# Attention through a small memory, fused with a two-layer ReLU-squared network: batches 2 to 7 form memory and scores for eight heads at once

## The chip, the cores and the metric

The kernel runs on one core of a Trainium2 chip. The metric is device time in microseconds; three runs of the kernel before gave 746.95, 749.21 and 749.82, median 749.21.

## What is computed

```
a    = softmax over the 576 tokens of phi              # 8 batches, 8 heads, 32 memories
k_m  = einsum('bhsm,bhsd->bhmd', a, k)                 # 32 x 64 for each head
v_m  = einsum('bhsm,bhsd->bhmd', a, v)
attn = softmax over the 32 memories of (q @ k_m^T / 8)
x    = attn @ v_m, heads side by side                  # 4608 x 512
out  = (relu(x @ w_in) ** 2) @ w_out                   # 512 -> 2048 -> 512
```

All inputs and the output are float32.

## The kernel before

Two products carry nearly all of the work. The attention output is never formed: `vw` (line 754) multiplies the value memory with the rows of `w_in` of each head, and `mm1` (line 864) multiplies the result with the attention weights of a batch, which gives the hidden layer directly. `mm2` (lines 899, 900, 902) and `mm2_left` (line 925, the tokens left over) multiply the squared hidden layer with `w_out`. These main products run in fp32r on high and low parts: `ath`/`atl`, `gh`/`glo`, and two parts of `w_out`. A program float32 matmul stands as two records in the trace, an fp32r one as one.

The small products run in plain float32. In batches 2 to 7 `memory(b, hh)` works on four heads at a time, so twice per batch. 128 partitions hold four tokens each, and 64 of them one more; `fold` takes the maximum and later the sum over these in three DVE instructions (lines 562 to 564). A transpose (570), a DVE maximum (572) and a second transpose (573) give the maximum over all tokens, which DVE subtracts (574); ACT takes the exponential (576). Line 594 sums over the tokens, line 582 forms keys and values in 128x32 tiles of TensorE, four at a time, over five groups of tokens (20 matmuls of 128 columns). After scaling, two transposes (625, 629) turn the result into `kb` and `VT`. One tile `KV` holds the inputs of a half; it is loaded again for each half. `scores` (793) then runs four times per batch, for four heads and 256 or 320 tokens each: two matmuls in 128x64 tiles.

Batches 0 and 1 use another form of the scores (`attention_turned`) and share the decoding of the weights with it. They run first, while the inputs and the weights are loaded. Their first main product waits for all of this; until then PE is kept busy with `idle` matmuls of zeros (`fill`, line 454).

The whole program is written down as a list of operations with their tiles. `Plan.order` then lets a planner put each operation on an engine and in an order. It counts with costs per operation and ranks taken from the table `PLACES` for the first operations and from its own rounds for the rest. What comes out is fixed: each engine runs its own list in order, SP too, which issues all loads. An operation whose input isn't there holds up all that stands behind it on its engine. PSUM has four banks `acc`, two `h`, and one each `pa` and `pv`; `vw` takes `pa` and `pv`, memory and scores of batches 2 to 7 take `pa` alone.

Of the kernel before, what the change touches and what calls it, by code (L numbers as in the profile page):

```python
# [20 lines left out]
P = 128  # L21
# [16 lines left out]
AHEAD = 2000  # L38
BEGIN = {"PE": 1000.0, "DVE": 1100.0, "ACT": 800.0, "POOL": 2100.0, "SP": 800.0}
# [79 lines left out]
class Buf:  # L119


    def __init__(self, plan, tag, slot, make, before):
        self.plan, self.tag, self.slot, self.make, self.before = plan, tag, slot, make, before
        self.tile = None
        self.users = []
        self.written = {}
        self.read = {}
        self.closed = False

    def __call__(self):  # L130
        if self.tile is None:
            self.tile = self.make()
        return self.tile


class Op:
    __slots__ = ("ways", "fn", "deps", "users", "late", "cap", "left", "start", "gap", "lead", "port", "size", "seq", "slack", "code")


class Plan:  # L140

    def __init__(self):
        self.ops = []
        self.slots = {}
# [205 lines left out]
def tt(n):  # L355
    return 68 + 1.04 * n
# [714 lines left out]
```

## Time and profile before

| | |
|---|---|
| median of three runs | 749.21 us |
| the profiled execution | 749.23 us, its span 747.3 us |
| PE busy | 733.1 us (98%) |
| DVE busy | 513.4 us (69%) |
| ACT busy | 311.1 us (42%) |
[...]
| moved by DMA | 66.38 MB |

Matmuls overlap, so the time that one takes from the next is read from start to start: in an undisturbed run of fp32r matmuls of 512 columns that is 0.231 us, of 256 columns 0.120, of 320 columns 0.146.

### The profile page before, as it was taken

The numbers are of one execution on the slowest core, as the hardware profiler recorded it, in microseconds if no ns is written. First come the engines' busy times: TensorE is split into PE (matmuls) and PEld (weight loads), VectorE is DVE, ScalarE is ACT, GpSimd is POOL, SyncE is SP. The second block draws the span as 40 slices with busy tenths as digits, with TensorE's granted clock in tenths as the row PEclk, the third lists the DMA queues.
The fourth block names the chain that finished last, engine by engine and source line by source line (L and its number), as shares of the span: only waits on it lengthen the run. The fifth ranks groups of instructions, "written<-read, shape, count | busy, mean of one in ns | idle before, by whom it ended". The sixth has DMA issues, their size and how long they took to land.

```text
span 747.3 us, 13089 instructions
## 1 busy us (share of the span) xinstructions
PE 733.1 (98%) x5004; PEld 586.9 (79%) x5009; DVE 513.4 (69%) x1200; ACT 311.1 (42%) x723; POOL 56.6 (8%) x132
## 2 busy tenths in 40 slices
PE   7899999999999999999999999999999999999997
PEld 4568888888878887788868888687877888788886
DVE  4889998944677677846767666955677576775551
ACT  3467997845422323523423323423242342443320
POOL 2000000010010000400014000120003200040000
PEclk9999999999999999999999999999999999999999
DMA  9994545260640036400363015410344102220002
GB/s 235 239 255 115 167 145 144 89 172 16 171 148 17 1 81 152 104 1 1 106 154 90 1 52 135 105 46 1 80 115 120 36 1 65 61 58 0 1 1 70
DMA packets 59997, 66.38 MB, mean 89 GB/s; under 512 B 18400, under 2 KB 48096, under 8 KB 59936
## 3 DMA queue, kind: packets, MB, share of 16 engines
q1 hardware_dynamic: 55904, 56.77, 30.0%
q0 software_dynamic: 3552, 8.13, 4.2%
q8 instruction: 39, 0.64, 0.4%
q10 hardware_dynamic: 480, 0.66, 0.4%
q14 instruction: 22, 0.18, 0.1%
HBM read 56.10 MB, written 9.44 MB: 88 GB/s over the span
## 4 chain that ended last, share of the span: by engine, by line
PE 92%; DMA 1%; ACT 0%; DVE 0%; issue 0%; ACTq 0%
PE h L864 28%; PE acc L899 16%; PE acc L902 16%; PE acc L900 16%; PE accl L925 6%; PE vwpv L754 4%; PE psc L793 2%; PE pkv L582 2%; DMA raw<-in_moe_w_out_dram 1%; PE psc L710 1%; PE pq L682 0%; PE vwpa L754 0%; PE pvt L625 0%; PE pvt L629 0%; PE pkv L594 0%; PE pmx L570 0%
## 5 line engine op out<-in xcount | busy, mean ns | idle before, releaser
L864 PE MATMUL h<-ath,vw 128*128 128x320 f32 (+1 forms) x1024 | 208.9, 298 | 0.9 <-ACT r L868 0.9
L899 PE MATMUL acc<-wo,gh 128*128 128x512 f32 x512 | 205.4, 401 | 0.0
L900 PE MATMUL acc<-wo,gh 128*128 128x512 f32 x512 | 201.0, 393 | 0.0
L864 PEld LDWEIGHTS h<-ath,vw 128*128 128x128 f32 x1024 | 168.6, 189 | 29.2 <-issue 7.2
L902 PE MATMUL acc<-wo,glo 128*128 128x512 f32 x512 | 159.9, 399 | 0.0
L870 ACT ACTIVATE gh<-r 128x512 fp32r<-128x512 f32 x128 | 81.0, 633 | 151.3 <-DVE r L869 116.2
L899 PEld LDWEIGHTS acc<-wo,gh 128*128 128x128 f32 x512 | 96.3, 188 | 28.2 <-issue 8.1
L902 PEld LDWEIGHTS acc<-wo,glo 128*128 128x128 f32 x512 | 91.9, 189 | 24.7 <-issue 7.5
L900 PEld LDWEIGHTS acc<-wo,gh 128*128 128x128 f32 x512 | 96.5, 188 | 17.2
L864 PE MATMUL h<-atl,vw 128*128 128x320 f32 (+1 forms) x512 | 109.5, 295 | 0.0
L869 DVE TENSOR_SCALAR r<-h 128x256 f32<-128x256 f32 (+1 forms) x104 | 47.4, 456 | 75.2 <-PE h L864 74.4
L868 ACT ACTIVATE r<-h 128x256 f32<-128x256 f32 (+1 forms) x152 | 61.2, 410 | 89.2 <-PE h L864 80.3
L874 DVE TENSOR_TENSOR glo<-r,gh 128x512 fp32r<-128x512 f32 x128 | 88.0, 687 | 13.7 <-ACT r L872 9.7
L864 PEld LDWEIGHTS h<-atl,vw 128*128 128x128 f32 x512 | 82.3, 189 | 0.0
L873 DVE TENSOR_TENSOR r<-r 128x576 f32<-128x576 f32 x69 | 52.2, 757 | 28.9 <-ACT gl L871 26.4
L961 POOL DMA_DIRECT2D out_dram<-o x84 | 41.4, 501 | 195.8 <-ACT o L428 187.4
L925 PE MATMUL accl<-wo,gl 128*128 128x512 f32 x192 | 48.0, 396 | 0.0
L925 PEld LDWEIGHTS accl<-wo,gl 128*128 128x128 f32 x192 | 35.5, 188 | 11.5 <-issue 4.0
L872 ACT ACTIVATE r<-r 128x576 f32<-128x576 f32 x59 | 40.5, 686 | 1.2
L754 PE MATMUL vwpv<-wi,VT 64*32 64x512 f32 (+1 forms) x264 | 34.9, 588 | 0.7 <-DVE wi L510 0.7
L754 PE MATMUL vwpa<-wi,VT 64*32 64x512 f32 (+1 forms) x264 | 34.9, 588 | 0.0
L871 ACT ACTIVATE gl<-r 128x64 fp32r<-128x64 f32 x128 | 31.5, 246 | 4.8 <-DVE r L869 4.5
(133 smaller groups left out, 700.9 us busy)
## 6 DMA issues: line engine op xcount, KB each, us to landing
raw<-in_moe_w_out_dram SPq DMA_DIRECT2D x16, 512.0 KB, 3.6
KV<-in_v_dram SPq DMA_DIRECT2D x16, 512.0 KB, 5.6
KV<-in_k_dram SPq DMA_DIRECT2D x16, 512.0 KB, 4.3
raw<-in_moe_w_in_dram SPq DMA_DIRECT2D x32, 256.0 KB, 4.3
q<-in_q_dram SPq DMA_DIRECT2D x24, 304.0 KB, 4.4
q<-in_q_dram SPq DMA_DIRECT2D x24, 240.0 KB, 3.9
out_dram<-o POOLq DMA_DIRECT2D x80, 64.0 KB, 2.0
phi<-in_phi_dram SPq DMA_DIRECT2D x16, 256.0 KB, 5.7
```

The lines of the kernel that those rows point to most:

```text
L754: nc.tensor.matmul(ps_[hh]()[32 * s:32 * s + 32, 0:n], V()[pr, s, :], W()[pr, s, c0:c0 + n], start=True, stop=True, tile_position=(64 * hh ...
L864: nc.tensor.matmul(p()[:, 0:n], V()[:, l, hh, c0:c0 + P], x()[:, hh, cs], start=(i == 0), stop=(i == 5))
L868: op({"ACT": act(n), **({} if b < 2 else {"DVE": tt(n)})}, lambda e, cs=cs, n=n, p=p: nc.scalar.activation(r()[:, cs], p()[:, 0:n], AF.Rel ...
L869: else nc.vector.tensor_scalar(r()[:, cs], p()[:, 0:n], 0.0, None, ALU.max), [p], [(r, h)])
L870: op({"ACT": act(SM)}, lambda e: nc.scalar.activation(gh(), r()[:, 0:SM], AF.Square), [r], [gh])
L873: else nc.vector.tensor_mul(r(), r(), r()), [r], [r], port=BOTH)
L874: vec({"DVE": tt(SM)}, lambda e: nc.vector.tensor_sub(glo(), r()[:, 0:SM], gh().bitcast(F32)), [r, gh], [glo])
L899: nc.tensor.matmul(a(), gh()[:, c], t()[:, 0], start=f0, stop=False)
L900: nc.tensor.matmul(a(), gh()[:, c], t()[:, 1], start=False, stop=False)
L902: nc.tensor.matmul(a(), glo()[:, c], t()[:, 0], start=False, stop=f1)
L925: nc.tensor.matmul(a(), G()[:, l, :], t()[:, w], start=(ff == 0 and n == 0), stop=(ff == NFF - 1 and n == 2))
L961: d(rows, o()[32 * j:32 * (j + n), :])
```

## The change

Memory of batches 2 to 7 takes all eight heads in one go. 64 partitions hold heads 0 to 3, the other 64 hold heads 4 to 7, nine tokens to a partition. Keys and values are formed in 64x32 tiles, eight at a time, over nine groups of tokens, in two instalments (five groups, then four) that share the one tile `KV`. Maximum and sum over the nine tokens are one DVE instruction each, which reads with a stride of 32 elements. The second transpose of the maximum becomes two matmuls in 128x64 tiles (`spread`). One pair of transposes yields keys and values of all heads. Scores take eight matmuls in 64x32 tiles with 288 tokens, twice per batch. They use `pa` and `pv`. The loads of q go to 32 partitions each, four to a tile. `mm1` cuts its 576 tokens into 288 and 288, not 256 and 320. The old memory function stays for batches 0 and 1 as `memory_half`, with keys and values as separate products of 64 columns and the maximum in one DVE instruction.

The planner's rounds go: ranks for all operations come from one table (its rows are not shown), and its cost of a PE operation now has a term for a change of tile shape (`SWITCH`) as well as other figures.

```diff
@@ order
-        rank = {o: PLACES[o.seq] * 10.0 if o.seq < len(PLACES) else best[1][o] for o in self.ops}
-        for _ in range(ROUNDS):
-            found = self.forward(rank)
...
+        rank = {o: PLACES[o.seq] for o in self.ops}
+        self.last, start, engine, gap = self.forward(rank)
@@ forward
+                t += SWITCH[mode][o.mode]
+                mode = o.mode
@@ sizes
-    CUT = (0, 8, NC)
-    TOK = (slice(0, 256), slice(256, S))
+    HC = NC // 2
+    RC = S // 64
+    KC = 5
+    TOK = (slice(0, S // 2), slice(S // 2, S))
@@ memory of batches 2 to 7
+    def rows(d, dst, src, lo, hi):
+        w = src.shape[3]
+        for x in (0, 1):
+            d(dst[64 * x:64 * x + 64].rearrange("p h c w -> p h (c w)"),
+              src[0, 4 * x:4 * x + 4].rearrange("h (p c) w -> p h (c w)", c=RC)[:, :, lo * w:hi * w])
+    def memory(b):
+        A = st([P, 4 * RC * M], F32, "phi", f"phi{b}")
...
+        vec({"DVE": tt(4 * RC * M)}, lambda e: nc.vector.tensor_reduce(
+            mx().rearrange("p (h m) -> p h m", h=4), a().rearrange("p h c m -> p h m c"), AX.X, ALU.max), [A], [mx], port=None, lead=True)
...
+        def spread(e):
+            for x in (0, 1):
+                nc.tensor.matmul(pm()[64 * x:64 * x + 64, P:2 * P], mc()[:, x].broadcast_to([P, 64]), ident, start=True, stop=True, tile_position=(0, 64 * x))
...
+        def sums(e):
+            for x in (0, 1):
+                pr = slice(64 * x, 64 * x + 64)
+                nc.tensor.matmul(pk[x]()[:, SUM:SUM + 1], asum()[pr], ones[pr], start=True, stop=True, tile_position=(64 * x, 0))
+        def products(pairs, lo, hi):
+            for c in range(lo, hi):
+                for h in range(4):
+                    for x in (0, 1):
+                        pr = slice(64 * x, 64 * x + 64)
+                        for o, src in pairs:
+                            nc.tensor.matmul(pk[x]()[32 * h:32 * h + 32, o], a()[pr, h, c, :], src(pr, h, c - lo),
+                                             start=(c == 0), stop=(c == RC - 1), tile_position=(64 * x, 32 * h))
...
+        for lo, hi in ((0, KC), (KC, RC)):
+            KV = st([P, 8 * KC * D], F32, "KV", f"KV{b}_{lo}")
...
@@ scores
+    def scores(b):
...
+            for y in (0, 1):
+                Q = st([P, 2, HC, D], F32, "q", f"q{b}_{h}_{y}")
...
+            pq = [pt(x + ".0", f"psc{x}{b}_{h}") for x in ("pa", "pv")]
+            def mm(e, qT=qT, pq=pq):
+                for s in range(4):
+                    for hh in (0, 1):
+                        pr = slice(64 * hh, 64 * hh + 64)
+                        nc.tensor.matmul(pq[hh]()[32 * s:32 * s + 32, 0:32 * HC], kb()[pr, 0, s, :], qT()[pr, s].rearrange("p c t -> p (c t)"),
+                                         start=True, stop=True, tile_position=(64 * hh, 32 * s))
```

PE, where batch 2 forms keys and values, before: after six `h` matmuls of the batch in progress stand the sum (594) and the twenty products of the first half (582); a second such block for the other heads follows 41 rows later.

```order
L864 MATMUL h_1_2280<-ath_366,vw_6_2098 128x320 x2
L594 MATMUL pkv_0_2288<-ones,asum_0_2272 128x1
L582 MATMUL pkv_0_2288<-KV_0_1970,phi_0_626 32x128 x20
L902 MATMUL acc_4_0_2123<-wo_1451,glo_2201 128x512
L902 MATMUL acc_4_3_2059<-wo_1399,glo_2248 128x512
```

The same place now: `pa` holds heads 0 to 3 and `pv` heads 4 to 7, and forty products of the first five groups take turns between the two banks.

```order
L916 MATMUL h_1_2347<-ath_380,vw_6_2157 128x288 x2
L565 MATMUL pkv_pa<-ones,asum_2336 128x1
L565 MATMUL pkv_pv<-ones,asum_2336 128x1
L573 MATMUL pkv_pa<-KV_0_2044,phi_881 32x128
L573 MATMUL pkv_pv<-KV_0_2044,phi_881 32x128
L573 MATMUL pkv_pa<-KV_0_2044,phi_881 32x128
L573 MATMUL pkv_pv<-KV_0_2044,phi_881 32x128
```

The products of the last four groups stand after 7.3 us of main products, counted at the start-to-start times above (7.2 to 7.6 in the six batches). From `spread` to the sums it is 4.7 to 8.7 us.

PE at the first scores of batch 2, before: two matmuls for the first 256 tokens of four heads, and after some main products two for the next 320.

```order
L900 MATMUL acc_4_3_2059<-wo_1771,gh_2402 128x512
L793 MATMUL psc_0_0_2491<-qT_0_0_1999,kb_2350 64x256 x2
L902 MATMUL acc_4_3_2059<-wo_1771,glo_2419 128x512
L864 MATMUL h_0_2497<-ath_366,vw_7_2174 128x256 x2
L864 MATMUL h_0_2497<-atl_378,vw_7_2174 128x256 x2
```

Now eight matmuls stand together for 288 tokens of all heads.

```order
L954 MATMUL acc_4_3_2159<-wo_1868,glo_2498 128x512
L848 MATMUL pscpa_0_2539<-qT_0_2076,kb_2524 32x288
L848 MATMUL pscpv_0_2541<-qT_0_2076,kb_2524 32x288
L848 MATMUL pscpa_0_2539<-qT_0_2076,kb_2524 32x288
L848 MATMUL pscpv_0_2541<-qT_0_2076,kb_2524 32x288
...
L916 MATMUL h_0_2550<-ath_380,vw_7_2271 128x288 x2
```

Four score places of a batch became two; between the two stand 8.3 to 9.9 us of main products, and between the second and the first `vw` 1.6 to 2.1.

SP, the loads around batch 2's last q, before: the inputs of one half of batch 3 (k, v, then phi), then the q tiles of batch 2's second half.

```order
L533 DMA KV_0_1970<-in_k_dram 128x4x256
L534 DMA KV_0_1970<-in_k_dram 64x4x64
L533 DMA KV_0_1970<-in_v_dram 128x4x256
L534 DMA KV_0_1970<-in_v_dram 64x4x64
L533 DMA phi_1_2453<-in_phi_dram 128x4x128
L534 DMA phi_1_2453<-in_phi_dram 64x4x32
L784 DMA q_1_0_2508<-in_q_dram 64x2x480 x2
L784 DMA q_1_1_2557<-in_q_dram 64x2x608 x2
```

Now (KV_5 is the second instalment of batch 2, KV_0 the first of batch 3, q_1_1 the last q tile of batch 2):

```order
L838 DMA q_1_0_2167<-in_q_dram 32x2x544 x4
L533 DMA KV_5_2419<-in_k_dram 64x4x256 x2
L533 DMA KV_5_2419<-in_v_dram 64x4x256 x2
L533 DMA KV_0_2510<-in_v_dram 64x4x320 x2
L533 DMA phi_2519<-in_phi_dram 64x4x288 x2
L533 DMA KV_0_2510<-in_k_dram 64x4x320 x2
L838 DMA q_1_1_2574<-in_q_dram 32x2x544 x4
```

The last q tile of a batch, 0.56 MB, moved behind 1.90 MB of the next batch (before 1.48 MB).

## Rows read from the trace of the kernel before

**Rows 1.** The page, busy time of each engine, share and instructions.

```profile
PE 733.1 (98%) x5004; PEld 586.9 (79%) x5009; DVE 513.4 (69%) x1200; ACT 311.1 (42%) x723; POOL 56.6 (8%) x132
```

**Rows 2.** Windows: stretch, length, busy time of PE, PEld, DVE, ACT, POOL, clock, DMA.

```profile
0.00:60.00 60.00, 50.97 (x606) 33.55 (x612) 45.49 (x118) 31.15 (x66) 5.56 (x23) 1.00 1.04 236
60.00:700.00 640.00, 639.10 (x4174) 517.71 (x4173) 449.20 (x1045) 271.07 (x636) 51.05 (x109) 1.00 0.30 79
700.00:747.30 47.30, 42.99 (x228) 35.61 (x226) 18.69 (x39) 8.89 (x23) 0.00 (x0) 1.00 0.10 28
```

**Rows 3.** PE by line: count, busy us, mean ns, idle before (zeros and transposes).

```profile
L454 PE MATMUL idle<-zero 128*128 128x512 bf16 x66 | 19.6, 428 | 1.5 <-DVE ones L444 1.0 <-issue 0.3
```

**Rows 4.** PE timeline at a transpose of the maximum: start, duration, instruction.

```profile
262.05 0.27 PE L573 MATMUL pmx<-ident,mc 128*128 128x128 f32 x1
262.08 0.47 PE L899 MATMUL acc<-wo,gh 128*128 128x512 f32 x1
262.39 0.40 PE L900 MATMUL acc<-wo,gh 128*128 128x512 f32 x1
```

**Rows 5.** PE timeline at keys and values of one half of batch 3.

```profile
266.71 0.28 PE L594 MATMUL pkv<-ones,asum 128*128 128x1 f32 x2
266.92 1.30 PE L582 MATMUL pkv<-KV,phi 128*32 128x128 f32 x40
268.15 1.19 PE L902 MATMUL acc<-wo,glo 128*128 128x512 f32 x4
269.18 0.39 PE L899 MATMUL acc<-wo,gh 128*128 128x512 f32 x1
```

**Rows 6.** PE timeline at scores of 256 tokens.

```profile
282.71 0.40 PE L902 MATMUL acc<-wo,glo 128*128 128x512 f32 x1
283.04 0.65 PE L793 MATMUL psc<-qT,kb 128*64 128x256 f32 x4
283.62 0.50 PE L899 MATMUL acc<-wo,gh 128*128 128x512 f32 x1
283.96 0.40 PE L900 MATMUL acc<-wo,gh 128*128 128x512 f32 x1
```

**Rows 7.** PE timeline at scores of 320 tokens.

```profile
286.14 0.76 PE L793 MATMUL psc<-qT,kb 128*64 128x320 f32 x4
286.83 0.56 PE L864 MATMUL h<-ath,vw 128*128 128x320 f32 x2
287.23 0.45 PE L864 MATMUL h<-atl,vw 128*128 128x320 f32 x2
```

**Rows 8.** PE timeline at a vw block: sixteen records in 64x32 tiles.

```profile
302.13 0.39 PE L900 MATMUL acc<-wo,gh 128*128 128x512 f32 x1
302.45 0.61 PE L754 MATMUL vwpv<-wi,VT 64*32 64x512 f32 x1
...
303.47 0.50 PE L899 MATMUL acc<-wo,gh 128*128 128x512 f32 x1
303.81 0.40 PE L900 MATMUL acc<-wo,gh 128*128 128x512 f32 x1
```

**Rows 9.** PE timeline at the start-up: forty records of one column.

```profile
42.11 0.51 PE L591 MATMUL pkv<-ones,phi 128*32 128x1 f32 x40
```

**Rows 10.** DVE and ACT by line: batches 0 to 7, three steps of memory and scores.

```profile
L574 DVE TENSOR_TENSOR phi<-phi,pmx 128x640 f32<-128x640 f32 x16 | 13.0, 815 | 4.2 <-PE pmx L573 4.1
L805 DVE TENSOR_REDUCE red_None<-S 128x18 f32<-128x576 f32 x12 | 9.0, 751 | 0.3
L576 ACT ACTIVATE phi<-phi 128x640 f32<-128x640 f32 x16 | 11.8, 740 | 40.9 <-DVE phi L574 30.9 <-issue 9.8
```

**Rows 11.** DMA of 266 to 276 us: issues, KB each, median us to landing.

```profile
KV<-in_k_dram SPq DMA_DIRECT2D x1, 512.0 KB, 4.7
```

**Rows 12.** DMA of 0 to 58 us in sum, then PE where batch 1's last q lands.

```profile
DMA packets 16283, 14.03 MB, mean 242 GB/s; under 512 B 5220, under 2 KB 14237, under 8 KB 16277
57.95 1.04 PE L682 MATMUL pq<-ident,q 128*128 128x128 f32 x8
```

More of the change, by code (lines that the diff above doesn't have):

```diff
@@ L38 @@
 AHEAD = 2000
+SWITCH = (
+    (0, 10, 85, 85, 85),
+    (90, 0, 85, 85, 85),
+    (100, 60, 0, 85, 85),
+    (100, 60, 85, 0, 85),
+    (100, 60, 85, 85, 0),
+)
 BEGIN = {"PE": 1000.0, "DVE": 1100.0, "ACT": 800.0, "POOL": 2100.0, "SP": 800.0}
@@ L136 @@
 class Op:
-    __slots__ = ("ways", "fn", "deps", "users", "late", "cap", "left", "start", "gap", "lead", "port", "size", "seq", "slack", "code")
+    __slots__ = ("ways", "fn", "deps", "users", "late", "cap", "left", "start", "gap", "lead", "port", "size", "seq", "slack", "code", "mode")
 class Plan:
@@ L199, in order @@
     def order(self):
-        for o in reversed(self.ops):
-            e = min(o.ways, key=o.ways.get)
-            cost = FIRST + o.size / WIRE + LANDS[e] if o.size else o.ways[e] + LAT[e]
-            late = min((u.late for u in o.users), default=1e9)
-            if o.cap is not None:
-                late = min(late, o.cap)
-            o.late = late - cost
-        rank = {o: o.late - (LEAD if o.lead else 0) for o in self.ops}
-        best = None
-        for _ in range(ROUNDS):
-            found = self.forward(rank)
-            if best is None or found[0] < best[0]:
-                best = found
-            rank = self.backward(found)
-        rank = {o: PLACES[o.seq] * 10.0 if o.seq < len(PLACES) else best[1][o] for o in self.ops}
-        for _ in range(ROUNDS):
-            found = self.forward(rank)
-            if found[0] < best[0]:
-                best = found
-            rank = self.backward(found)
-        self.last, start, engine, gap = best
+        rank = {o: PLACES[o.seq] for o in self.ops}
+        self.last, start, engine, gap = self.forward(rank)
         for o in self.ops:
@@ L428, in copy, with dma @@
         nc.scalar.copy(o, i) if e == "ACT" else ENG[e].tensor_copy(o, i)
-    def dma(fn, size, r=(), w=(), eng="SP", two=False, **more):
+    def dma(fn, size, r=(), w=(), eng="SP", two=False, issue=None, **more):
         e = {"SP": nc.sync, "ACT": nc.scalar, "POOL": nc.gpsimd}[eng]
-        issue = 700 if eng == "POOL" else 1250 if two else 620
+        issue = issue or (700 if eng == "POOL" else 1250 if two else 620)
         return op({eng: issue}, lambda _: fn(e.dma_start), r=r, w=w, size=size, **more)
@@ L587, in sums @@
-        def sums(e):
-            if asum is None:
-                for c in range(SC):
-                    for s in range(4):
-                        nc.tensor.matmul(pk()[32 * s:32 * s + 32, 2 * D:2 * D + 1], a()[:, s, c, :], ones,
-                                         start=(c == 0), stop=(c == SC - 1), tile_position=(0, 32 * s))
-            else:
-                nc.tensor.matmul(pk()[:, 2 * D:2 * D + 1], asum()[:, 0:P], ones, start=True, stop=True)
-        op({"PE": 180 if asum else 530}, sums, [asum or A], [pk], lead=True, code=4 if asum else 82)
@@ L629, in memory, with mm @@
-        op({"PE": 60}, lambda e: nc.tensor.transpose(pv()[:, 0:P], two(1), ident), [kx if b < 2 else (kx, 1)], [(pv, 0)], lead=True)
-        pr = slice(64 * hh, 64 * hh + 64)
-        op({"ACT": act(P), "DVE": tt(P)}, lambda e: copy(e, VT[b]()[pr].rearrange("p h m -> p (h m)"), pv()[pr, 0:P]), [(pv, 0)], [(VT[b], hh)], lead=True)
+        def mm(e, i):
+            for c in range(SC):
+                for s in range(4):
+                    nc.tensor.matmul(pk()[32 * s:32 * s + 32, i * D:i * D + D], a()[:, s, c, :], kv()[:, i, s, c, :],
+                                     start=(c == 0), stop=(c == SC - 1), tile_position=(0, 32 * s))
@@ new lines, in memory_half @@
+        for i in (0, 1):
+            op({"PE": 700}, lambda e, i=i: mm(e, i), kin + [(KV, i), (KV, "pad")], [(pk, i)], lead=True, code=82, mode=3)
+            op({"ACT": act(P), "DVE": 75 + 1.04 * P}, lambda e, i=i: nc.scalar.activation(kx()[:, i], dup(i), AF.Copy, scale=rs()[:, 0:1]) if e == "ACT"
+               else nc.vector.tensor_scalar_mul(kx()[:, i], dup(i), rs()[:, 0:1]), [(pk, i), rs], [(kx, i)], lead=True)
+        pv = pt(bank, f"pvt{u}")
+        kb = kTs[b, hh] = st([P, 4, 2, M], F32, "kb", f"kb{u}", 2)
@@ new lines, in memory_half @@
+        op({"POOL": 250}, lambda e: nc.gpsimd.memset(kb(), 0.0), [], [kb], lead=True)
+        two = lambda i: kx()[:, i].rearrange("p r d -> p (r d)")
+        op({"PE": 30}, lambda e: nc.tensor.transpose(pv()[:, P:2 * P], two(0), ident), [(kx, 0)], [(pv, 1)], lead=True, mode=1)
+        for x in (0, 1):
+            pr = slice(64 * x, 64 * x + 64)
+            op({"ACT": act(P), "DVE": tt(P)}, lambda e, x=x, pr=pr: copy(e, kb()[pr, :, x, :], pv()[pr, P:2 * P].rearrange("p (h m) -> p h m", h=4)),
+               [(pv, 1), kb], [(kb, x)], lead=True)
@@ L633, in attention_turned @@
+        vt = VT[b][0]
+        po = slice(64 * hh, 64 * hh + 64)
+        op({"PE": 30}, lambda e: nc.tensor.transpose(pv()[:, 0:P], two(1), ident), [(kx, 1)], [(pv, 0)], lead=True, mode=1)
+        op({"ACT": act(P), "DVE": tt(P)}, lambda e: copy(e, vt()[po].rearrange("p h m -> p (h m)"), pv()[po, 0:P]), [(pv, 0)], [(vt, hh)], lead=True)
     def attention_turned(b):
@@ L816, in attention, with load @@
-    def attention(b, split=False):
-        S_ = [scores(b, hh, split) for hh in (0, 1)]
-        i = b % 2 if b < 2 else (b + 1) % 2
+            qT = st([P, 4, HC, 32], F32, "qT", f"qT{b}_{h}")
+            for y in (0, 1):
+                Q = st([P, 2, HC, D], F32, "q", f"q{b}_{h}_{y}")
+                def load(d, Q=Q, h=h, y=y):
+                    for hh in (0, 1):
+                        src = q[b, 4 * hh + 2 * y:4 * hh + 2 * y + 2].rearrange("a (p c) d -> p a (c d)", c=NC)
+                        for x in (0, 1):
+                            lo = h * HC * D + 32 * x
+                            d(Q().rearrange("p a c d -> p a (c d)")[64 * hh + 32 * x:64 * hh + 32 * x + 32, :, 0:HC * D - 32], src[:, :, lo:lo + HC * D - 32])
+                dma(load, P * 2 * (HC * D - 32) * 4, [], [Q], issue=2500, lead=True)
+                vec({"DVE": 48 + 1.13 * 64 * HC}, lambda e, qT=qT, Q=Q, y=y: nc.vector.transpose(qT()[:, 2 * y:2 * y + 2], Q()[:, :, :, 0:32]), [Q], [(qT, y)], port=None, lead=True)
@@ L819, in attention @@
+        return S_
+    def attention(b):
+        S_ = scores(b)
+        i = (b + 1) % 2
         ah, al = att[b] = (st([P, 2, S], F32R, f"ath{i}", f"ath{b}"), st([P, 2, S], F32R, f"atl{i}", f"atl{b}"))
```

308 lines of the change are left out of this document (120 added, 188 removed), and 212 rows, old and new, of the table PLACES.

## The prediction

> **What bounds the kernel now.** I read the busy times first: PE 733.1 of 747.3 us, DVE 513.4, ACT 311.1 [rows 1]. Then where PE is not busy: 9.0 us of the first 60, 0.9 us of the next 640, 4.3 us behind the last matmul [rows 2]. The granted clock is 1.00 in every stretch. In the first 60 us the DMA engines are full (share 1.04), and 66 matmuls of zeros, 19.6 us busy, stand in for work [rows 2, 3]. So there are two regimes. In the start-up the loads set the time, at 242 GB/s [rows 12]. From 60 us on nothing but PE's own instructions does, and a microsecond less on PE is a microsecond less of the span, as long as nothing else becomes late. The profiled execution took 749.23 us, its span 747.3; the median of the three runs is 749.21, so the sum is made from 749.2. A measurement of this kernel tells a change from none at about 0.5%, 3.7 us.
>
> **PE work removed in batches 2 to 7.** Costs are taken from start to start, over the 0.231 us (512 columns) or 0.146 us (320) that a main product takes undisturbed.
> A transpose: 262.05 to 262.39 is 0.34, less 0.23, so 0.11 us [rows 4].
> Keys and values of one half: 266.71 to 269.18 is 2.47, less four times 0.231, so 1.54 us, of which 0.11 is the sum (a transpose's price) and 1.43 the twenty products [rows 5].
> Scores of 256: 282.71 to 283.96 is 1.25, less two times 0.231, so 0.79 us [rows 6]. Its wait ahead is 0.33 less 0.23, 0.10.
> Scores of 320: 286.14 to 287.23 is 1.09, less 0.29 for the two main products, plus the same 0.10 ahead, so 0.90 us [rows 7].
> A vw block: 302.13 to 303.81 is 1.68, less 0.46, so 1.22 us for 512 columns [rows 8].
> All of these lie on one line: 0.37 us for each block plus 1.66 ns for each column streamed through a tile (0.79 for 256, 0.90 for 320, 1.22 for 512; 0.37 + 640 x 1.66 ns = 1.43 for five groups of 128). It holds for 128x32, 128x64 and 64x32 tiles alike, so the number of tiles that run beside each other is free, and 64x32 tiles do eight at a time in a vw block.
> Before, per batch: 8 transposes 0.88, two halves of keys and values 3.08, scores 2 x 0.79 + 2 x 0.90 = 3.38. Sum 7.34 us.
> After: one transpose 0.11; `spread`, 128 columns in two tiles, 0.58; two transposes at the end 0.22; five groups 1.43; four groups, 512 columns, 1.22; scores twice 288 columns, 2 x 0.85 = 1.70. The sums now have a tile shape of their own, 64x128: between 0.11, as before, and 0.31, with a change of shape on each side at the 0.10 of rows 6; I take 0.2. Sum 5.46 us. So 1.9 us less per batch, over six batches **11.3 us**.
> Bounds: no row has eight tiles with only 128 columns in each. If all sixteen records of a group hide behind its 0.21 us of columns, the price stands. The nearest row for the issue of short records is forty of one column, busy 0.51 us [rows 9], 12.8 ns each; sixteen at that rate are 0.20 us, just under the 0.21 us. At worst I allow a tenth more per group, 0.2 us per batch, 1.2 us in all. `spread` has as its nearest row from below the transpose that it replaces, 0.11: 2.8 us the other way.
> `mm1` in 288 and 288 columns instead of 256 and 320 streams the same columns with the same count of matmuls: nothing.
>
> [...]
>
> **Loads of batches 2 to 7.** Two of them stand closer to their use. A lone load of 0.52 MB landed 4.7 us after its issue [rows 11]; at 242 GB/s [rows 12] 2.2 us of that is the data, 2.5 fixed.
> The second instalment of keys and values, 1.05 MB, can only be issued when the first block has read the tile: 2.5 + 4.3 = 6.8 us later it is there. PE has 7.2 to 7.6 us of main products between the blocks and 0.2 us of changes of shape. Nothing, with 0.6 us to spare.
> The last q tile stands on SP behind 1.90 MB for the next batch, which start when the second block has read `KV` and `phi`. The 2.46 MB land 2.5 + 10.2 = 12.7 us after that block. Score 2 starts, by the order and the prices above, 13.1 to 14.8 us after it. Between stand a DVE transpose of 576 elements (0.73 us, scaled from the subtraction's 0.815 for 640 [rows 10]) and 0.3 us that I allow for handovers: it must land by 12.1 to 13.8. Over the five batches that have a successor that is late by 0, 0.6, 0, 0.6, 0.5: 1.7 us. But the 242 GB/s hold 5220 packets of 16283 under 512 B [rows 12], and the new loads have none (1,024 to 2,176 B). At 260 GB/s nothing is late. I take **0.8 us**, bounds 0 and 1.7 at these rates; slower loads are a rival.
>
> **The chain from `spread` to the sums.** DVE subtracts 1152 elements, ACT takes the exponential, DVE sums. Scaled from rows 10 that is 0.815 x 1.8 + 0.740 x 1.8 + 0.751 x 2 = 4.3 us, an upper figure since each has a fixed part; main products of 4.7 to 8.7 us cover it. The strided sum has no row. As fast as the contiguous one it costs nothing; at twice its time, 1.5 us more, four of the six batches (4.7 to 5.3 us of cover) would lose 0.5 to 1.1 us each, 3.5 us. I take 0.3 us for this and the waits for `pa` and `pv`: between score 2 and `vw` 1.6 to 2.1 us cover two DVE transposes of 288 elements (0.4 us each, scaled from rows 10) and the handovers. Behind a late sum stand PE's main products, which nothing else can overtake.
> DVE loses some 140 instructions; PE waited for it nowhere after 60 us [rows 2], so that gives nothing.
>
> **Start-up.** By SP's order the last load that batch 1 waits for, its second q, came after 12.98 MB and now comes after 13.50 (two `w_in` pieces went ahead of it). PE took it up at 57.95 [rows 12], so now at 60.1 (0.52 MB at 242 GB/s is 2.2 us). Ahead of it PE had 5.7 us of main products and now has 7.2. Net 0.7 us lost. Keys and values in separate products of 64 columns cost between -0.3 (bound by issue, 0.51 each) and +1.3 us per half for batches 0 and 1; mostly this lies in time that PE spends waiting for loads. I take **0.7 us** for all, bounds -1.5 and 3.
> The end is the same 48 matmuls, an evacuation and a store: the 4.3 us stay.
>
> **Sum.** 749.2 - 11.3 + 0.8 + 0.3 + 0.7 = **739.7 us**.
>
> **Rivals.**
> Late loads, moderate. The loads to 64 and 32 partitions run at some 210 GB/s: the q tile lands 14.2 us after the block, late by 1.1, 2.1, 0.4, 2.1 and 2.0, and the second instalment by 0.1 in six batches. That is 8.3 us in place of the 0.8, so 747: no change. For it: these loads have more issues (four for a q tile, before two). Against it: loads to 64 partitions were part of the 242.
> Late loads, strong, the other side. The place is the same q tile and the second instalment. From about 205 GB/s downwards the two together eat the gain; at 170 GB/s the tile lands 17.0 us after the block, on the mean 4.3 us late in five batches, and the second instalment 1.3 us late in six: 29 us, so 768. Against it: no stretch of full DMA in the trace is that slow.
> Floor per record, from the issue side. If a record costs twice the 12.8 ns of the row of forty because eight tiles need twice the weight loads of four, sixteen are 0.41 us, the nine groups 3.7 instead of 1.9, 10.6 us in all: 751, no change. Against it: the sixteen records of a vw block follow the same line as the others [rows 8].
> A better start-up. The new order may cut into the 19.6 us of zeros instead of adding to them: 3 us less, and no late loads, 736.
>
> **Chances.** Forecast 0.70 (736 to 743.5 on its own terms); better start-up 0.13; moderate lateness 0.09; floor per record 0.04; strong lateness 0.04. Faster by over 0.5% takes the forecast, the better start-up and a third of the moderate case, 0.86; the same is the rest of that case and the floor, 0.10; slower is the strong lateness, 0.04. The range 735.0 to 744.5 takes in the bounds of the sum (a saving of 10 to 13, lateness of 0 to 1.7, start-up -1.5 to 3) short of all of them at once.
>
> **What would show it.** Right: per batch one block of 40 program products of about 1.4 us and one of 32 of about 1.2, two score blocks of 0.85, PE busy from 60 us on with under 3 us idle, the first q wait of batch 1 near 60 us, and no idle time of PE behind DVE's strided sum. Wrong: idle time of PE ended by a load of q or KV, blocks of keys and values above 2 us, or more than 36 us of zeros and idle time ahead of 62 us.

## The result, and the profile after

| | before | after |
|---|---|---|
| median of the runs | 749.52 us (4 runs, 746.95 to 750.04) | 759.14 us (4 runs, 756.92 to 760.97) |
| ratio, 95% interval | | 1.0139 [1.0113, 1.0166] |
| profiled execution, its span | 749.23, 747.3 | 756.92, 755.1 |

The forecast was 739.7 us, faster by 9.5. The kernel became slower by 1.4%. The profiled executions differ by +7.7 us.

The page of after, busy time of each engine, against [rows 1]:

```profile
PE 731.2 (97%) x5637; PEld 582.4 (77%) x5641; DVE 499.4 (66%) x1062; ACT 322.4 (43%) x742; POOL 53.7 (7%) x116
```

PE is busy 1.9 us less than before, in a span 7.8 us longer. Two of the windows of [rows 2], and two short ones (stretch, length, busy time of PE, PEld, DVE, ACT, POOL, clock, DMA share, GB/s):

```profile
0.00:60.00 60.00, 48.09 (x719) 31.43 (x724) 43.17 (x100) 28.32 (x62) 4.84 (x18) 0.94 0.88 231
60.00:700.00 640.00, 631.93 (x4663) 507.58 (x4662) 434.12 (x919) 283.87 (x658) 48.81 (x98) 1.00 0.32 80
20.80:24.20 3.40, 2.54 (x42) 1.87 (x32) 2.28 (x8) 1.33 (x5) 1.09 (x3) 0.50 1.07 235
51.60:54.90 3.30, 3.30 (x36) 3.11 (x27) 0.38 (x1) 2.22 (x8) 0.00 (x0) 0.50 0.92 305
```

Two things are new. Between 60 and 700 us PE is idle for 8.1 us, where it was idle for 0.9. And in the start-up there are two stretches with a granted clock of 0.50, where each window of [rows 2] has 1.00. In the second PE is busy all of the time; ahead of it, it stood still for 2.6 us (below).

What ended PE's waits in after, over the whole span (instruction, releaser: idle us, times, longest):

```profile
PE pscpa L848 <- DVE qT L841: 4.0, 3, 2.0
PE h L916 <- issue: 2.6, 1, 2.6
...
PE acc L954 <- DVE glo L926: 2.2, 3, 1.2
```

The first is the score block of a late q tile. The second has no releaser: a stop in the first products of `h`, at 47 us. The third is a main product that waits for its input.

Where the time went I read at equal work: the times at which both kernels have as many main products (`h`, `acc`, `accl`, 3264 in each) behind them. After is 2.2 us late at its first (46.39 us), 5.2 at 80 us, about 7.1 at 150 us (neighbouring products differ by about 1 us there, as their order differs) and 8.2 at the last. From 150 us on the batches' own products, and what PE waits for them, are measured as in the prediction, from start to start over the undisturbed spacing:

| term, us | forecast | measured |
|---|---|---|
| small products of batches 2 to 7 | -11.3 | -9.9 |
| waits of score blocks (6.3) and second key and value block (1.8) | +0.8 | +8.1 |
| chain to the sums | +0.3 | +0.6 |
| `acc` waits for `glo` | 0 | +2.2 |
| start-up, to 150 us | +0.7 | +7.1 |
| tail | 0 | -0.3 |
| sum (the spans differ by 7.9) | -9.5 | +7.8 |

**The work is nearly as small as forecast.** PE by line and form, keys and values of heads 0 to 3 in batches 2 to 7 (176 to 755 us; count, busy us, mean ns, idle before):

```profile
L573 PE MATMUL pkv_pa<-KV,phi 64*32 64x128 f32 x432 | 16.2, 273 | 0.1
```

With as many records for heads 4 to 7 that is nine groups of sixteen per batch; before, two halves took five groups each. One score block without a wait, the first of batch 3 (PE timeline: start, us, instruction; sixteen records in all):

```profile
290.96 0.40 PE L952 MATMUL acc<-wo,gh 128*128 128x512 f32 x1
291.29 0.43 PE L848 MATMUL pscpa<-qT,kb 64*32 64x288 f32 x1
...
291.93 0.53 PE L916 MATMUL h<-ath,vw 128*128 128x288 f32 x2
292.30 0.43 PE L916 MATMUL h<-atl,vw 128*128 128x288 f32 x2
```

0.33 us to the block less 0.23 for the main product, 0.64 for the block, and 0.37 less 0.27 for the return: 0.84 us, forecast 0.85. The two `h` halves of 288 take 0.133 us each, together what 256 and 320 took.

**The second block of the same batch waits for q.** PE (the product behind the second key and value block, then the score block), then DVE, then SP's queue in the stretch before it:

```profile
288.45 0.50 PE L954 MATMUL acc<-wo,glo 128*128 128x512 f32 x1
...
301.54 0.43 PE L848 MATMUL pscpa<-qT,kb 64*32 64x288 f32 x1
...
303.53 0.43 PE L848 MATMUL pscpa<-qT,kb 64*32 64x288 f32 x1 [1.30 <-DVE qT L841]
304.15 0.51 PE L954 MATMUL acc<-wo,glo 128*128 128x512 f32 x1
```

```profile
302.70 0.78 DVE L841 STREAM_TRANSPOSE qT<-q 128x576 f32<-128x576 f32 x1 [3.92 <-DMA q<-in_q_dram]
```

```profile
288.60 1.25 SPq L533 DMA_DIRECT2D phi<-in_phi_dram  x2
...
292.94 2.55 SPq L838 DMA_DIRECT2D q<-in_q_dram  x4
```

The second key and value block ends at 288.45. At once SP starts the next batch's `phi` and `KV`, 1.9 MB, and only then this batch's last q. It lands at 302.62, DVE turns it, and the block takes 2.61 us instead of 0.65. Its four DMA issues (KB each, us to landing), and the window in which the DMA engines are full:

```profile
q<-in_q_dram SPq DMA_DIRECT2D x4, 136.0 KB, 8.5
```

```profile
291.00:301.00 10.00, 10.00 (x66) 8.09 (x65) 7.25 (x11) 3.06 (x8) 0.00 (x0) 1.00 1.10 228
```

The tile lands 14.2 us after the block, forecast 12.7. At 228 GB/s the 2.46 MB take 10.8 us of it (forecast 10.2), which leaves 3.4 for issue and fixed part (forecast 2.5). In batches 3, 4, 5 and 6 this costs 1.96, 0.21, 1.35 and 2.67 us.

**VectorE waits too.** A wait of DVE at 214 to 218 us, on the next batch's `phi`:

```profile
DVE mx L543 <- DMA phi<-in_phi_dram: 4.3, 1, 4.3
```

Behind it on DVE stands the current expert's `glo`, for which PE then waits: the 2.2 us of `acc` above.

**The start-up.** PE at its stop, with the granted clock still 1.00 ahead of it and 0.50 from 51.5 us on:

```profile
46.76 0.42 PE L916 MATMUL h<-atl,vw 128*128 128x288 f32 x2
47.03 0.43 PE L916 MATMUL h<-ath,vw 128*128 128x288 f32 x2
50.06 0.53 PE L916 MATMUL h<-ath,vw 128*128 128x288 f32 x2 [2.61 <-issue]
52.76 0.68 PE L916 MATMUL h<-atl,vw 128*128 128x288 f32 x2
53.24 0.44 PE L916 MATMUL h<-ath,vw 128*128 128x288 f32 x1
```

Two such products are 0.27 us apart at a granted clock of 1.00 (46.76 to 47.03), and 0.48 at 0.50 (52.76 to 53.24). Nothing that the products need is late. In 47.2 to 50.1 us the DMA queues show one read that is not data, of 16 KB (packets, MB, share), begun at 47.35:

```profile
q8 instruction: 1, 0.02, 2.9%
```

Ahead of the stop stands the densest run of records in the kernel, sums and products of two halves in batches 0 and 1, now separate for keys and values: 160 records from 43.87 us to 46.39, of which the first group is

```profile
43.87 0.49 PE L653 MATMUL pkv<-ones,phi 128*32 128x1 f32 x39
```

### The profile page after: what moved, and what is told of

The parts are those of the page before. It is cut to its first block, busy times and chain, and to the rows that moved or that the text cites. A ratio compares the mean times of both kernels' runs of the same rounds, so it can differ in the third digit from the quotient of the medians.

```text
span 755.1 us, 14141 instructions
## 1 busy us (share of the span) xinstructions
PE 731.2 (97%) x5637; PEld 582.4 (77%) x5641; DVE 499.4 (66%) x1062; ACT 322.4 (43%) x742; POOL 53.7 (7%) x116
## 4 chain that ended last, share of the span: by engine, by line
PE 81%; DVE 7%; DMA 6%; ACT 2%; issue 2%; SPq 1%; DVEq 0%; ACTq 0%
PE h L916 24%; PE acc L954 14%; PE acc L951 14%; PE acc L952 13%; PE accl L977 6%; DMA q<-in_q_dram 4%; PE vwpv L808 4%; PE pkv_pa L573 1%; PE pscpa L848 1%; DMA raw<-in_moe_w_in_dram 1%; SPq L838 1%; DVE qT L841 1%; PE pkv L659 1%; PE pkv_pv L573 1%; DMA KV<-in_k_dram 1%
## 5 line engine op out<-in xcount | busy, mean ns | idle before, releaser
L916 PE MATMUL h<-ath,vw 128*128 128x288 f32 x1024 | 213.0, 299 | 3.7 <-issue 2.6
L954 PE MATMUL acc<-wo,glo 128*128 128x512 f32 x512 | 183.6, 400 | 2.2 <-DVE glo L926 2.2
L954 PEld LDWEIGHTS acc<-wo,glo 128*128 128x128 f32 x512 | 94.4, 188 | 29.7 <-issue 6.7
L916 PE MATMUL h<-atl,vw 128*128 128x288 f32 x512 | 109.9, 296 | 0.0
L920 ACT ACTIVATE r<-h 128x288 f32<-128x288 f32 x153 | 61.1, 409 | 95.1 <-PE h L916 51.5
L921 DVE TENSOR_SCALAR r<-h 128x288 f32<-128x288 f32 x103 | 46.8, 457 | 44.3 <-PE h L916 42.2
L927 DVE TENSOR_TENSOR gl<-r,gl 128x64 fp32r<-128x64 f32 x128 | 27.6, 219 | 16.1 <-ACT r L924 14.8
L435 ACT CAST vw<-vwpa 128x256 fp32r<-128x256 f32 x51 | 18.8, 375 | 45.7 <-PE h L916 26.9
```

The source lines that it names most:

```text
L916: nc.tensor.matmul(p()[:, 0:n], V()[:, l, hh, c0:c0 + P], x()[:, hh, cs], start=(i == 0), stop=(i == 5))
L920: op({"ACT": act(n), **({} if b < 2 else {"DVE": tt(n)})}, lambda e, cs=cs, n=n, p=p: nc.scalar.activation(r()[:, cs], p()[:, 0:n], AF.Rel ...
L921: else nc.vector.tensor_scalar(r()[:, cs], p()[:, 0:n], 0.0, None, ALU.max), [p], [(r, h)])
L954: nc.tensor.matmul(a(), glo()[:, c], t()[:, 0], start=False, stop=f1)
```

## The experiments

The theory after the first profile: 8.1 us of the miss are loads behind which q, and the second instalment, stand in SP's queue; 7.1 are the start-up, by its order or by its small records. Fifteen kernels follow. The median of before beside them was 747.6 to 748.6 us; all intervals are against it.

### Loads: e1, e5, e8

SP's order behind batch 3's second instalment, in after and in the two kernels that move its loads (b is 3; batches 2 to 6 alike):

```
after            e1               e5
phi (b+1)        q last (b)       phi (b+1)
KV v (b+1)       phi (b+1)        q last (b)
KV k (b+1)       KV v (b+1)       q first (b+1)
q last (b)       KV k (b+1)       KV v (b+1)
q first (b+1)    q first (b+1)    KV k (b+1)
```

> The changed kernel with one thing moved: on SP the loads of the next batch (its phi, 0.59 MB, and its first keys and values, 1.31 MB) stand behind the load of the batch's last q tile instead of ahead of it, for batches 2 to 6. Theory A (last q tile is late because it waits on the DMA engines behind these 1.90 MB): the four waits inside the second score block of a batch (1.96, 0.21, 1.35 and 2.67 us, 6.2 us in all) go, every score block takes 0.65 us, and the time falls from 759.1 to about 753 (751.5 to 754.5). Rival B (the transpose of the tile comes late by VectorE's own queue, or by the single q slot, whatever the load does): the waits stay within 1 us of what they are, 758 to 760. Rival C (the moved loads now come late for the next batch): new waits ended by phi or by the first keys and values, 759 or more.

e1 took 788.77 us, 1.0551 [1.0505, 1.0596]: much slower than after. The score blocks no longer wait in five of six batches. But q's tile comes free late, at 299.5 in batch 3, and as SP works in order, `phi` behind it starts 12.8 us later than in after (301.37 against 288.60). PE's waits, then DVE's from 200 to 330 us:

```profile
PE acc L1028 <- DVE glo L1000: 17.1, 4, 7.6
PE pscpa L922 <- DVE qT L915: 7.8, 1, 7.8
```

```profile
DVE mx L617 <- DMA phi<-in_phi_dram: 15.8, 2, 9.8
```

DVE takes the maximum over `phi` well ahead of its use, and everything queued behind it on DVE waits too. Behind these waits PE's clock falls to 0.50 in five stretches of 3.4 to 6.9 us, 27.3 us in all, so the 38 us against e5 are not waits alone. So `phi` must stay in front, and only `KV` go behind q.

> The changed kernel, on SP: the next batch's phi (0.59 MB) stays where it is, ahead of the last q tile, and only its first keys and values (1.31 MB) go behind the last q tile and the next batch's first q tile. In the first trial phi went too; there the waits in the second score block went in five batches of six, but VectorE, which takes its work in order, stood at the maximum over the next batch's phi for up to 9.8 us, and TensorE behind it. Theory A (the second score block waits for the 1.31 MB): waits in the score blocks fall from 6.2 us to under 1 us, VectorE waits no longer for phi than in the changed kernel; 759.1 - 5.5 = about 753.5 (752 to 755). Rival B (what the last q tile gains, another load in the order loses: the keys and values or the next q tile come late for their own users): 757 to 761.

e5 took 750.91 us, 1.0029 [1.0013, 1.0046], 8.2 less than after. SP, the landing of q, and the same score block as above:

```profile
287.74 1.25 SPq L607 DMA_DIRECT2D phi<-in_phi_dram  x2
292.10 8.44 SPq L912 DMA_DIRECT2D q<-in_q_dram  x8
300.58 1.26 SPq L607 DMA_DIRECT2D KV<-in_v_dram  x2
```

```profile
q<-in_q_dram SPq DMA_DIRECT2D x4, 136.0 KB, 2.7
```

```profile
300.70 0.43 PE L922 MATMUL pscpa<-qT,kb 64*32 64x288 f32 x1
...
301.35 0.50 PE L1028 MATMUL acc<-wo,glo 128*128 128x512 f32 x1
```

The tile lands 2.7 us after issue instead of 8.5, the block takes 0.65 us, and the waits for `glo` are down to 0.2 us. At equal work e5 is 9.5 us shorter than after from 154 us on: of the 8.1 us of waits at the blocks 1.1 stay, and those for `glo` go too, which theory A had left out (it expected 752 to 755). So the loads theory holds. The start-up is 2.6 us later than that of after, with PE's products in the same order.

e8 puts the second key and value block, its transposes and the first score block three PE operations later, in e7 (below):

> As the kernel with all three moves, and in batches 2 to 7 the products with the second part of keys and values, the transposes behind them and the first score block stand three steps of main products (some 1.5 us) later on TensorE. The second load lands some 8.2 us after the block that frees its tile and the products come 7.2 to 7.5 us after it: theory A says the waits inside that block (1.8 us over six batches) go, 1 to 2 us less than the kernel with three moves. Rival B: the later scores put a wait of the same size behind them, no difference within 1 us.

It took 746.45 us, 0.9973 [0.9957, 0.9989]; e7 took 743.47. The second key and value blocks are all without a wait now, but a score block waits in their place (it takes 1.11 us in batch 5), and so do main products, so nothing is won there. Its start-up is 2 to 3 us worse than that of e7 though PE's order there is the same; a wait for the first `KV` is 3.1 us, not 1.9, and the clock is at 0.50 from 22.5 to 29.3 us, which that of e7 never is in its start-up. What sets off either was not settled.

### Start-up: e2, e6, e10

e2 keeps the operations of after but takes, up to 150 us of plan, the order of before. e6 keeps the order of after but forms keys and values of batches 0 and 1 in one product again, 160 records fewer:

```diff
-        def mm(e, i):
+        def mm(e):
...
-                    nc.tensor.matmul(pk()[32 * s:32 * s + 32, i * D:i * D + D], a()[:, s, c, :], kv()[:, i, s, c, :],
+                    nc.tensor.matmul(pk()[32 * s:32 * s + 32, 0:2 * D], a()[:, s, c, :], kv()[:, :, s, c, :],
```

> The operations of the changed kernel, all of them, but up to 150 us of the plan in the order (and on the engine) that the kernel before gives them; from there the changed kernel's order. At equal amounts of main products the changed kernel is 7.1 us late by 166 us. Theory A (the order of the start-up makes this: the dense run of small products at 43.9 us, the stop of 2.6 us behind it, the half clock after that): the first 166 us come out within 2 us of the kernel before, total about 752 to 753. Rival B (the operations of batches 0 and 1 make it: keys and values in products of their own, one phi tile for both halves, so that batch 1's phi must wait for both halves of batch 0): most of the 7 us stays, 757 to 760.

> The changed kernel with the products of keys and values of batches 0 and 1 in one record of 128 columns each, as in the kernel before, instead of two of 64 columns: 160 records (320 instructions with their weight loads) fewer in the first 60 us; the order is the changed kernel's. Theory A (the start-up loses its time to the fetch of instructions, 2.6 us of a bare stop at 47.2 us, and to the half clock behind it, because the dense small records run through the code faster than it comes): the stop goes or shrinks, start-up 2 to 5 us shorter, 754 to 757. Rival B (the split is free, the stop stands elsewhere again): 758 to 760.

e2: 758.25 us, 1.0149 [1.0116, 1.0183]. e6: 759.06, 1.0133 [1.0106, 1.0160]. Neither alone gains anything in all. Stops without a releaser, one of 1.6 us at `pkv` in e6 and these in e2:

```profile
PE h L990 <- issue: 4.2, 1, 4.2
PE pkv L727 <- issue: 1.4, 1, 1.4
```

The clock of e6 is at 0.51 from 20.8 to 24.2 us, as in after. e10 does both:

> The two moves of the start-up without that of the loads: the kernel before's order up to 150 us and keys and values of batches 0 and 1 in one record; from there the changed kernel as it is, its loads too. The order alone gave 758.3 and the one record alone 759.1, neither of them a gain. If the start-up needs both (with one of them a stop for instructions or a half clock stays): 743.5 + 6 to 8 = about 751 (749 to 753). If the 7.4 us between the kernel with the loads moved (750.9) and that with all three moves come from the loads in some other way: 756 to 759.

753.23 us (five runs, 751.14 to 757.02), 1.0078 [1.0048, 1.0108], 5.9 less than after. In its profile (752.13 us) the start-up is 1.3 us ahead of before at 100 to 144 us, with no stop and a mean clock of 1.00:

```profile
0.00:60.00 60.00, 51.71 (x617) 34.65 (x622) 48.43 (x115) 32.39 (x68) 4.69 (x18) 1.00 0.92 229
```

So either the order of after or its split products are enough to lose most of the 7.1 us. The profiles bear this out: at equal work, at 120 us, the seven kernels with the order of after are 5.5 to 11.1 us later than before (after 6.1, e6 with one product 5.5), e2 and e3 (old order, split products) 5.3 and 5.0, and the five with the old order and one product that far (e7, e8, e10, e13, e15) -1.3 to 2.2. Where the old order ends, at 154 to 166 us, some 3 us are lost again in e2, e7 and e10; the total of e2 hides that its start-up gains 0.8 us on after at 120 us.

### Place and zeros: e4, e16, e12, e13, e11

The stops fall where nothing is late, so the place of the instructions themselves was shifted, by matmuls of one column ahead of the first zeros (64 of them, 32 in e16). They compute nothing that is used:

```diff
+                for _ in range(64):
+                    nc.tensor.matmul(idle[:, 0:1], zero.broadcast_to([P, P]), zero, start=True, stop=True)
```

> The changed kernel with 64 more matrix products of one column each, into the idle bank, at the very start, where TensorE waits for its first loads: they cost under 1 us there and move every later instruction of TensorE by 128 places. Theory A (the stop of 2.61 us at 47.2 us, in which TensorE waits for nothing in the profile, is the fetch of TensorE's next 16 KB of instructions, which the trace shows on queue 8 at 47.35 us): the stop goes or stands at another product, and with it the half clock at 51.5 us; total 755 to 758, or as before if another stop takes its place. Rival B (the stop belongs to that product, by some wait the profile does not name): it stays at the same main product with about 2.6 us, total 759 to 760.

> The changed kernel with 32 such products at the start instead of 64: another place of its instructions. If its start-up loses its 7 us at any place (its order and its split records make the stop, the place only moves it): 757 to 761, with a stop of 2 us or more or a half clock ahead of 60 us. If the place alone makes it, some shift is free of both: 752 to 755.

e4 is after with 64: 758.49 us (one of four runs 753.57), 1.0131 [1.0092, 1.0171]. The stop at `h` is gone, another of 2.2 us stands at 15 to 17 us, and the clock of 0.50 lasts 13.6 us, with PE busy for 12.3 of them:

```profile
18.60:32.20 13.60, 12.30 (x161) 9.85 (x163) 8.89 (x21) 5.10 (x12) 1.41 (x4) 0.50 0.63 167
```

e16 is after with 32: 762.19 us, 1.0200 [1.0166, 1.0235], a stop of 3.6 us at `pkv` and one of 1.5. The stop stands at another product; the loss stays.

> The kernel before, unchanged but for 64 products of one column at the very start, as was done to the changed kernel (there the first main product came 6 us later and the granted clock was at half for 13.7 us, while the stop for instructions at 47 us was gone). If the quiet start-up of the kernel before is a matter of where its instructions fall and of the clock, it loses 2 to 8 us too: 751 to 757. If its order bears such a shift: 748 to 750.

> The kernel with all three moves (743.5 us), with 64 products of one column at the very start, the shift that cost the kernel before 2.7 us (751.3 against 748.6 or so) and left the changed kernel's total where it was. If the quiet start-up of that kernel is partly luck, as the kernel before's is: a stop of 2 us or more that nothing explains around 47 us, and a half clock; 746 to 749. If its order is quiet at any place of its instructions: 743 to 745.

e12 is before with 64: 751.28 us, 1.0033 [1.0015, 1.0051]. e13 is e7 with 64: 746.12, 2.6 more than e7. The profiles of both show what after had, a stop at `h`, of 3.4 us in e13, and in e12:

```profile
PE h L864 <- issue: 2.3, 1, 2.3
```

and e12 a stretch at a clock of 0.50 that before has not:

```profile
21.90:28.70 6.80, 4.79 (x48) 3.54 (x50) 4.00 (x10) 1.81 (x3) 0.70 (x2) 0.50 1.11 208
```

The quiet start-up of before is therefore in part the place of its instructions; by the medians some 3 us, which would leave about 4 of the 7.1 for order and split, an estimate. The place does not settle it alone. e12 ran from 747.20 to 754.15 us, and its profile is of the slowest of ten runs; its three runs with a mean clock of 1.000 took 747.2 to 748.6, as before does. e13 ran from 742.12 to 747.91, its profile is of a run of 747.74, and its fastest run beats every one of e7. After lost at each of the three places tried (758.5 to 762.2 us).

e11 adds 18 zeros at four places in the start-up of after (16 to 24, 1 to 4 twice, 6 to 10), to keep the clock up:

> The changed kernel with 18 more products on zeros at four places of its first 32 us where TensorE stands idle for 0.8 to 2 us (8 before the first transpose, 3 each before the first scores and the second pair of transposes, 4 before the first hidden weights). The granted clock of the changed kernel falls to half at 20.8 us for 3.4 us and at 51.5 us for 3.4 us; in the kernel before it never does. Theory A (the idle time ahead sets it off): no half clock at 20.8 us, first main product at 45 us instead of 46.4, total 757 to 758. Rival B (the half clock at 20.8 us costs nothing, since TensorE waits for others there): clock mended, time 759. Rival C: the clock falls all the same.

761.58 us, 1.0175 [1.0149, 1.0201]. The clock of 0.50 came all the same, twice as long:

```profile
20.60:27.40 6.80, 6.19 (x97) 4.48 (x97) 3.37 (x11) 2.30 (x7) 1.41 (x4) 0.50 1.10 230
51.30:58.10 6.80, 5.22 (x66) 4.52 (x65) 2.83 (x8) 3.74 (x10) 0.00 (x0) 0.50 0.31 80
```

**What the stops are.** Sixteen stops of over 1 us without a releaser stand in the start-ups of eleven of the seventeen profiles. The records ahead of them tell more than the product at which they stand. Windows up to the stop in after, e2 and e12 (x is the count of records, products behind PE, weight loads behind PEld):

```profile
0.00:47.40 47.40, 38.26 (x596) 23.02 (x600) 35.34 (x82) 19.32 (x39) 4.84 (x18) 0.96 0.98 251
0.00:45.80 45.80, 36.79 (x595) 22.32 (x600) 34.52 (x81) 18.26 (x35) 4.67 (x18) 1.00 1.02 254
0.00:49.80 49.80, 43.22 (x590) 28.02 (x596) 36.07 (x96) 20.35 (x41) 5.58 (x23) 0.93 1.05 239
```

In nine kernels (after, e1, e2, e3, e5, e11, e12, e13, e16) a stop of 2.3 to 4.2 us comes after 590 to 600 products, whatever product stands there; in e6 one comes after 471, and in six kernels one of 1.1 to 2.2 us after 219 to 221. The reads on the queue `q8` number 44 in after for 5,637 products and 39 in before for 5,004, so 128 products and their weight loads to a read of 16 KB. Each of the sixteen stops ends 2.5 to 2.9 us after such a read began (after: 47.35 and 50.06). The nine kernels reach the later place within 2.2 to 5.3 us of passing the 256 records ahead of it, the other eight (before, e4, e6, e7, e8, e9, e10, e15) take 7 to 16 us for these records and do not stop there, though such reads come in them too. The author's reading is that in the stops PE waits for its own instructions, which the dense small records use up before the next read lands. The place and the end of the stops speak for it; no run took the reads away, so it was not shown by itself.

### Both mended: e3, e7, e9, e15

> Both moves together: the kernel before's order up to 150 us, and the next batch's loads behind the last q tile. If each is right and they do not touch each other, the gains add: 759.1 - 6.2 - 6.5 = about 746.5 (745 to 748), a little faster than the kernel before (749.5). If only the loads matter, 753; if neither, 759.

e3 (e1 and e2): 790.98 us, 1.0578 [1.0549, 1.0607], e1's fault again.

> Three moves on the changed kernel: the kernel before's order up to 150 us, keys and values of batches 0 and 1 in one record as in the kernel before, and the next batch's first keys and values behind the last q tile. Start-up like the kernel before's within 2 us (first main product at 44 to 46 us, no stop of over 1 us that nothing explains), score blocks without waits. If the first two only trade one stop for another: 753; if both parts hold: 759.1 - 6 - 5.5 = about 747.5 (745 to 750).

e7 (e2, e5 and e6): **743.47 us, 0.9927 [0.9903, 0.9951]**, better than both kernels by its median, 15.7 us below after. e5 gave 8.2 and e10 5.9, 14.1 in all, so the two causes are separate in the main. Its start-up:

```profile
0.00:60.00 60.00, 51.81 (x616) 33.98 (x616) 47.80 (x114) 31.67 (x67) 4.67 (x18) 1.00 0.95 227
```

It still loses some 3 us at 144 to 191 us, where the two orders meet. So the meeting was put at 95 and at 120 us:

> The kernel with all three moves (743.5 us), but with the kernel before's order only up to 95 us of the plan instead of 150. At 150 us the two orders meet in the first steps of batch 2, and between 144 and 191 us that kernel lost 3 us at equal work (a wait of 1.8 us for the low half of the hidden products among them). If that loss belongs to the place where the orders meet: 740.5 (739 to 742). If batch 2 loses it wherever they meet: 743 to 744.

> The kernel with all three moves, the two orders meeting at 120 us of the plan instead of 150 (at 95 us TensorE waited 5.3 us for decoded weights there, and the total was 749.8; at 150 us 3 us are lost in the first steps of batch 2). If one of the two losses goes and the other does not come: 741 to 742.5. Otherwise 743.5 to 749.

e9: 749.79 us, 1.0019 [1.0004, 1.0034]. e15: 746.30, 0.9978 [0.9968, 0.9988]. Both are worse than e7: a `vw` block now waits for its weights, 3.5 us in e15, and in e9 as below. Behind it the clock is at 0.50 for 6.8 us in e9 (from 105.8 us) and 6.9 in e15 (from 131.8).

```profile
PE vwpv L882 <- DVE wi L582: 5.9, 2, 5.3
```

## Why the prediction was wrong

- **What bounds the kernel: right.** From 60 us on PE's own work and PE's waits add up to the difference [rows 2].
- **PE work removed: right but for a size.** -9.9 against -11.3 us. The law of 0.37 us and 1.66 ns per column held for `spread` (0.57, forecast 0.58) and the scores. The block of sums and five groups took 1.81 (1.63), that of four 1.29 (1.22): 0.25 us a batch more, within the worst cases kept for it (0.2 for the groups, 0.1 for the sums).
- **Floor per record: refuted.** A block of four groups costs 1.29 us where nothing waits; less the 0.37 per block that is 0.23 us for sixteen records, 14 ns each, where this rival had 0.41 us (its 751 us is 750.3 by its own terms).
- **Loads: this step failed.** 0.8 us forecast, 8.1 measured. The place (the last q tile, behind the next batch's `phi` and `KV`) and the need were right; the landing was not. It was reckoned at 12.7 us, from 2.5 fixed [rows 11] and 242 GB/s [rows 12], and came at 14.2, 0.6 by the rate and 0.9 by the fixed part. That is the moderate rival's landing, which gave 8.3 us in all (7.7 for q, 0.6 for the instalment; measured 6.3 and 1.8), with a chance of 0.09; that it meets it so well is partly luck, as it assumed 210 GB/s, and 228 were measured with a longer fixed part. With needs of 12.1 to 13.8 us the cost went from 1.7 to 8.3 within 1.5 us of landing time: a step so near its edge deserved a wide range, and taking 0.8 of 1.7 pushed it the wrong way. e5 shows the cause by taking it away.
- **What DVE waits for: not in the prediction.** It followed q and `KV`, not `phi`, whose maximum stands early in DVE's queue: 2.2 us of PE's time in after, and waits of DVE of up to 9.8 us in e1.
- **Chain to the sums: right**, 0.6 for 0.3; for the strided sum PE waited once, 0.2 us.
- **Start-up: this step failed too.** 0.7 us forecast, with a bound of 3, and 7.1 measured. The load on which the 0.7 rested came early: batch 1's last q was taken up at 58.07 us, near the 57.95 of [rows 12], not at 60.1. The prediction counted loads and columns. It priced the 160 records more by columns and issue, bounded by [rows 9], and took the granted clock of before [rows 2] for that of after. The runs show instead a stop behind dense records (2.6 us in after, over 2.7 us after a read on `q8` began), a clock of 0.50 for 3.3 us behind that, and that the order of after or its split products are each enough to keep most of the loss (at 120 us e6 is 5.5 us later than before, e2 5.3); both had to go to be rid of it (e10). The first main product's 2.2 us of delay, ahead of the stop, were not taken apart.
- **Signs.** Idle time ended by q and `KV` was named as a sign against the forecast, and came. More than 36 us of zeros and idle time ahead of 62 us did not come: it is 30 (before 29). Neither the stop of 2.6 us nor a PE that is busy longer at a clock of 0.50 brings it near 36, so that sign was blind to what happened.

Not settled: when a read of instructions begins, whether e12 and e13 stop in their faster runs too (one run of each is profiled), and what sets off the clock of 0.50 at 20 to 32 us. For the second stretch the order of events is plain: in the nine profiles with a stop of 2.3 us or more at 45 to 53 us the clock falls between 1.6 us before the end of the stop and 1.5 us after it (after: 50.06 and 51.54), and in the eight others it does not fall between 45 and 60 us. That the stop brings it is argued from this; no run took the stop away alone. The 18 zeros of e11 did not stand in the place of the stop.

## What to carry to other kernels

For a transfer into a tile that is the only one of its kind reckon with two times: when the tile is free, and what is queued ahead of it on its DMA queue by then (q landed 8.5 us after its issue in after, 2.7 in e5); where the margin is within the 1.5 us by which the landing was missed here (14.2 for 12.7), take the slower rate for the sum. Before moving a load past others, look at which in-order engine has the moved one early in its queue (e1 against e5: 38 us, by the waits above all for where `phi` stands). And a finer split of small products in a dense start-up can cost more than its columns: with the start-up order of before the 160 records more took 758.25 us for 753.23 (e2 against e10); try it with the start-up left as it was. Where an engine stops for nothing that the profile names, count its records up to the stop (590 to 600 in nine kernels) and look for a read of instructions (begun 2.5 to 2.9 us before the end of each stop).

## What the hardware showed that was not expected

- The number of small tiles cost nothing here: sixteen records in 64x32 tiles with 288 columns passed in 0.64 us, and four in 128x64 tiles with 256 columns took 0.58 [rows 6].
- 64 matmuls of one column ahead of the start-up make before 3.1 us slower and e7 2.6, 32 make after 3.0 slower, and 64 leave after as it was. The 64 take PE 1.9 us in e12, 29 ns each on the whole array, where forty of one column in 128x32 tiles took 12.8 ns each [rows 9]:

```profile
1.01 1.87 PE L1039 MATMUL idle<-zero 128*128 128x1 bf16 x64 [1.01 <-DVE ones L444]
```

- TensorE stopped sixteen times in the start-ups where nothing that the profile names was late: at 590 to 600, 471 or 219 to 221 products, and each stop was over 2.5 to 2.9 us after a read of 16 KB on `q8` began. That it waited for its own instructions is read from this.
- The granted clock was at 0.50 also in stretches in which PE was nearly always busy (3.3 of 3.3 us in after, 12.3 of 13.6 in e4); ahead of both PE had stood still, for 2.6 and 2.2 us.
- The clock of one kernel differs from run to run: of 69 runs of before beside the experiments the 21 with a mean clock of 0.999 or 1.000 took 747.2 us at the median, the 19 at 0.993 to 0.995 749.3.
